# A written order for five engines from the beginning to the first half layer, a folded projection, and lists of the other experts made later

## The chip, the cores and the metric

The kernel runs on one core of a Trainium2 chip. The time is that of one launch in device microseconds; the figure before is the median of three runs. TensorE is written PE, its weight loads PEld, VectorE DVE, ScalarE ACT, GpSimd POOL; SP is the queue that issues most of the transfers.

## The reference

`x` has 2048 tokens of 448 values. The layernorm of it, `xn`, feeds two branches, and the sum of both and of `x` is the output.

```
xn  = layernorm(x)
q   = (xn @ wq) as 16 heads of 28;  k = xn @ wk;  v = xn @ wv     # one key and value head of 28
A   = softmax(q k^T * 28**-0.5) v  ->  (2048, 448) @ wo
gates = softmax(xn @ wg)                    # 8 experts, the best 2 of each token, renormalized
B   = sum over its 2 experts of gate * (gelu(xn @ w1[e]) @ w2[e])  # 448 -> 1792 -> 448
out = x + A + B
```

## The kernel before

All products are carried out in parts: an operand is split into a rounded high part and the low remainder (`hi` on ACT, `lo` a subtraction on DVE or POOL), and a product of 448 rows is 11 matmuls: high by high 4, high by low 3, low by high 4 (`mm11`; the low parts of the last 64 rows ride in the free half of the fourth chunk).

**Prologue.** Sixteen tiles of 128 tokens are loaded (tiles `xn`), normalized (`norm`: statistics on DVE, square root and scaling on ACT, every fourth tile's scaling on POOL), written to DRAM for the gathers (`xn_d`), transposed on PE (L559) and split into `xh` and `xl`. Four tiles make a chunk of 512 tokens. For each chunk `project` multiplies by `wa`, the 64 columns of wk, wv and wg (L581, L583: 7 matmuls of 512 columns, high and low part side by side in 128 columns), copies the result (`pkv`), transposes it back (L588) and adds the two halves into `kvg`. `q_mm` makes a group of four heads, padded from 28 to 32 rows each (L54, 11 matmuls of 512 columns); there are 16 such groups, split by `q_out` and written to DRAM (`q_d`). The tiles are loaded first, then wq in four pieces.

**The gate.** From `kvg` DVE finds the two best experts of each token and counts ranks (`gate_rank`, a count by PE, L361 and L363); the lists of tokens of all eight experts are made at once: `gate_hot` makes one-hot rows `ob` and right-hand sides `rt` of 40 columns (DVE), `gate_tok` multiplies them (L403, 4 groups of 8 matmuls), the result is `tok`. Expert 0's rows are then gathered from `xn_d`, transposed (L240) and split.

**Experts.** An expert has 512 to 576 rows, in two halves (the second takes what is over 256). First layer: 14 steps `f` of 11 matmuls (for a first half 256 columns), gelu on ACT (`gf`, L891), split into `gg` (L35, L899). Second layer: for each group `k` of 128 rows 14 steps of 3 matmuls (L940) with `w2h` and `w2l`, the split pieces of w2. Between these steps `tock` lets in bursts of attention scores: 7 matmuls of 512 columns (L135) into `ps_s` and a half bank `ps_w`, whose maxima DVE takes (`mx`, L152), part of them from ACT's copy `cp`. Two PSUM tiles `ps_w0` and `ps_w1` take turns for the steps' results. The attention itself follows after the last expert.

**What sets the order.** Each engine executes its instructions in the order of the program. Tile, the scheduler, gives that order by priorities; inside a `manual_schedule` the order of the code stands for the engines named. Before, PE, DVE and ACT stand in such an order from the fourth query group to the end of the prologue, and PE from then on; the beginning is Tile's.

The lines that decide which tiles POOL normalizes and how many query groups stand between the projections:

```
moe_attention(..., npool=(3,), hr=50, early=(0, 1, 2, 1))
for ch in range(4):
    if ch < 3:
        norm(ch + 1)
    project(ch)
```

Of the kernel before, what the change touches and what calls it, by code (L numbers as in the profile page):

```python
# [30 lines left out]
EPS = 1e-5  # L31

# [9 lines left out]
def mm11(nc, out, wh, wl, xh, xl, w_is_lhs, between=None):  # L42

# [4 lines left out]
    for i, (a, b) in enumerate(pairs):  # L51
        if not w_is_lhs:
            a, b = b, a
        mm = nc.tensor.matmul(out, a, b, start=i == 0, stop=i == n - 1)  # L54
        if between and i == 2:
            between()
# [4 lines left out]
def moe_attention(ctx, tc, x, wq, wk, wv, wo, wg, w1, w2, out, hp=200, slow=0.4, first=0.9, fin=11, find=4,  # L61
                  npool=(3,), hr=50, early=(0, 1, 2, 1)):
# [7 lines left out]
    q_d = [[dram.tile([512, 512], F32, name=f"q{s}{c}_d") for c in range(4)] for s in "hl"]  # L70
# [16 lines left out]
    tok = cst.tile([128, E * 5], I32, name="tok")  # L87
# [31 lines left out]
    def s_query(t):  # L119
        SQ[t] = sS.tile([128, 4, 128], F32R, name="qs")  # L120
        nc.sync.dma_start(SQ[t].bitcast(F32), q_d[0][t // 4].rearrange("(g p) q -> p g q", g=4)
                          [:, :, (t % 4) * 128:(t % 4) * 128 + 128])
# [78 lines left out]

    def high_w1(pc, st):
# [5 lines left out]
    def low_w1(pc, st, a):  # L208
        b = wp1.tile([128, 4, 256], F32R, name="w1l", tag="w1l")
        lo(nc, b, st, a)  # L210
        W1[0, pc] = a, b

    W1 = {}

    def gather(e, i, xs):
        n = min(128, CAPS[e] - i * 128)
        it = tok[0:n, i * E:i * E + 1] if e == 0 else tokp[0:n, i, e:e + 1]
# [14 lines left out]
    X = {}  # L232
# [4 lines left out]
    def turn_x(e, i, xh, xl, n, xs, p):  # L237
        p = p.rearrange("p (c n) -> p c n", c=4)
        for c in range(4):
            tr = nc.tensor.transpose(p[:, c, 0:n], xs[0:n, c * 128:(c + 1) * 128], ident[0:n, 0:n])  # L240
        s = slice(i * 128, i * 128 + n)
        with tc.high_priority(offset=hp):
            hi(nc, xh[:, :, s], p[:, :, 0:n])
            if e == 0:
                lo(nc, xl[:, :, s], p[:, 0:3, 0:n], xh[:, 0:3, s])
                lo(nc, xh[64:128, 3, s], p[64:128, 3, 0:n], xh[64:128, 3, s])
            else:

                xt = xs.rearrange("p (c n) -> p c n", c=4)
                nc.scalar.activation(xt[:, :, 0:n], p[:, :, 0:n], AF.Copy)  # L250
        if e:
            for o, a, b in ((xl[:, :, s], xt[:, 0:3, 0:n], xh[:, 0:3, s]),
                            (xh[64:128, 3, s], xt[64:128, 3, 0:n], xh[64:128, 3, s])):
                nc.gpsimd.tensor_tensor(o, a, b.bitcast(F32), op=OP.subtract)
        if e == 0:
            trail.append(tr.ins.name)


    with ExitStack() as p0:
# [16 lines left out]

        def load_x(t):
# [978 lines left out]
```

## Time and profile before

| | us |
|---|---|
| median of 3 runs | 1396.79 (1396.76 to 1397.5) |
| profiled execution | 1399.3 |
| its span | 1397.6 |
| PE busy in it | 1366.5 (98%) |
| start to the first matmul of expert 0 | 85.67 |
| first layer of expert 0, first token half | 85.67 to 106.61 |
| second layer of it | 106.61 to 129.77 |

The profiled execution is one run under the profiler, 2.5 us above the median. In the rows, a stretch in square brackets is the idle time before an instruction and what ended it; rows of equal form that follow each other are merged.

### The profile page before, as it was taken

The page shows a single profiled execution, that of the slowest core. Times are in us where ns is not written, and L with a number is a line of the kernel's source. Part 1 is how long each engine was busy: PE and PEld are TensorE (multiplying, and loading weights), DVE is VectorE, ACT ScalarE, POOL GpSimd, SP SyncE. Part 2 cuts the span into 40 slices and gives each one's busy share as a digit, 9 for nine tenths or more (in the row PEclk, how much of TensorE's full clock was granted, in tenths as well). Part 3 has the DMA queues.
Part 4 walks back from the last instruction along what each step waited for, and adds up shares of the span by engine and source line. Part 5 has one row for each costly group of instructions (what it writes and reads, how often), then busy time and mean ns, then how long its engine had stood idle before and what let it go on. Part 6 is the DMA issues. An engine that isn't in the chain of part 4 may idle for free.

```text
span 1397.6 us, 27007 instructions
## 1 busy us (share of the span) xinstructions
PE 1366.5 (98%) x10809; PEld 903.4 (65%) x10809; DVE 753.9 (54%) x775; ACT 997.6 (71%) x1506; POOL 510.7 (37%) x461
## 2 busy tenths in 40 slices
PE   5999999999999999999999999999999999999997
PEld 4887888888788788788788886333333443333333
DVE  6678778778777877788787885211111111111112
ACT  6454674674665665656647645999999999999995
POOL 6010791882872864855838812000000000000000
PEclk9999999999999999999999999999999999999999
DMA  8862251350441341432523314111211122221110
GB/s 263 268 202 82 87 157 34 107 147 30 128 126 37 120 119 51 132 105 66 146 67 107 98 42 110 38 52 51 51 51 51 53 58 61 56 56 51 52 36 23
DMA packets 106495, 124.82 MB, mean 89 GB/s; under 512 B 14914, under 2 KB 94194, under 8 KB 106238
## 3 DMA queue, kind: packets, MB, share of 16 engines
q1 hardware_dynamic: 101278, 106.73, 25.8%
q0 software_dynamic: 5088, 16.32, 4.4%
q8 instruction: 86, 1.41, 0.5%
q14 instruction: 43, 0.35, 0.1%
HBM read 98.25 MB, written 24.77 MB: 88 GB/s over the span
## 4 chain that ended last, share of the span: by engine, by line
PE 92%; DMA 3%; DVE 2%; POOL 1%; ACT 1%; issue 1%; SPq 0%; POOLq 0%; ACTq 0%; DVEq 0%
PE ps_w L54 22%; PE ps_w L940 20%; PE ps_pv L1113 18%; PE ps_s L827 16%; PE ps_s L135 5%; PE ps_s L1035 3%; PE ps_w L135 2%; PE ps_p L54 2%; DMA st<-in_B_w_dram 1%; DMA xs<-xn_d,tokp 1%; PE ps_w L240 1%; PE ps_s L54 1%; POOL w1l L199 1%; PE ps_st L827 1%; DVE mx L152 0%
## 5 line engine op out<-in xcount | busy, mean ns | idle before, releaser
L152 DVE TENSOR_REDUCE mx<-ps_s 128x4 f32<-128x2048 f32 (+1 forms) x159 | 358.5, 2256 | 84.3 <-PE ps_s L135 83.9
L1105 ACT ACTIVATE P<-ps_s 128x512 f32<-128x512 f32 x510 | 282.5, 616 | 33.1 <-PE ps_st L827 28.6
L940 PE MATMUL ps_w<-w2h,gg 128*128 128x448 f32 (+1 forms) x966 | 293.7, 379 | 0.0
L143 ACT ACTIVATE cp<-ps_s 128x1024 f32<-128x1024 f32 x156 | 160.0, 1025 | 159.8 <-PE ps_s L135 125.6
L1113 PE MATMUL ps_pv<-P,vaug 128*32 128x512 f32 x2040 | 269.1, 604 | 0.0
L1105 ACT ACTIVATE P<-ps_st 128x1024 f32<-128x1024 f32 x255 | 268.9, 1055 | 0.0
L899 POOL TENSOR_TENSOR gg<-gf,gg 128x512 fp32r<-128x512 f32 (+2 forms) x140 | 147.4, 1065 | 280.6 <-ACT gg L35 259.2
L940 PEld LDWEIGHTS ps_w<-w2h,gg 128*128 128x128 f32 (+1 forms) x966 | 170.1, 186 | 45.4 <-issue 29.8
L1021 POOL DMA_INDIRECT yk<-y_d,slot x32 | 35.1, 1098 | 431.3 <-DVE xr L1026 424.5
L940 PE MATMUL ps_w<-w2l,gg 128*128 128x448 f32 (+1 forms) x518 | 189.9, 367 | 0.0
L152 DVE TENSOR_REDUCE mx<-cp 128x2 f32<-128x1024 f32 (+1 forms) x157 | 188.8, 1203 | 1.7 <-ACT cp L143 1.7
L827 PEld LDWEIGHTS ps_s<-qah,kT 32*128 32x128 f32 x514 | 47.6, 181 | 207.0 <-ACT P L1105 187.3
L54 PE MATMUL ps_w<-xeh,w1h 128*128 128x256 f32 (+2 forms) x896 | 165.8, 298 | 0.7 <-ACT gf L891 0.7
L54 PE MATMUL ps_w<-xeh,w1l 128*128 128x256 f32 (+2 forms) x896 | 147.8, 287 | 0.0
L54 PEld LDWEIGHTS ps_w<-xeh,w1h 128*128 128x128 f32 x896 | 128.9, 188 | 28.8 <-issue 19.0
L827 PE MATMUL ps_s<-qah,kT 32*128 32x512 f32 x514 | 128.5, 495 | 0.8 <-ACT P L1105 0.5
L827 PE MATMUL ps_st<-qah,kT 32*128 32x512 f32 x510 | 127.5, 495 | 0.0
L54 PEld LDWEIGHTS ps_w<-xeh,w1l 128*128 128x128 f32 x896 | 125.8, 188 | 0.0
L199 POOL TENSOR_TENSOR w1l<-st,w1h 128x1024 fp32r<-128x1024 f32 x49 | 117.3, 2400 | 8.4 <-ACT w1h L35 6.6
L54 PE MATMUL ps_w<-xel,w1h 128*128 128x256 f32 (+2 forms) x672 | 120.0, 287 | 0.0
L135 PE MATMUL ps_s<-kT,qs 28*128 28x512 f32 x939 | 115.2, 452 | 3.0 <-ACT mt L114 1.6
L891 ACT ACTIVATE gf<-ps_w 128x512 f32<-128x512 f32 (+2 forms) x145 | 74.1, 511 | 58.7 <-PE ps_w L54 55.1
(273 smaller groups left out, 2014.7 us busy)
## 6 DMA issues: line engine op xcount, KB each, us to landing
st<-in_B_w_dram SPq DMA_DIRECT2D x56, 448.0 KB
st<-in_B_w_dram SPq DMA_DIRECT2D x52, 384.0 KB
y_d<-y SPq DMA_DIRECT2D x32, 224.0 KB
st<-in_B_w_dram SPq DMA_DIRECT2D x104, 64.0 KB
xn_d<-xn SPq DMA_DIRECT2D x16, 256.0 KB
qh_d<-qh SPq DMA_DIRECT2D x16, 256.0 KB
ql_d<-ql SPq DMA_DIRECT2D x16, 256.0 KB
qs<-qh_d SPq DMA_DIRECT2D x16, 256.0 KB
```

What stands on the lines that cost most here:

```text
L54: mm = nc.tensor.matmul(out, a, b, start=i == 0, stop=i == n - 1)
L135: nc.tensor.matmul(p3 if k < 0 else p[:, k, :] if k < 4 else p2[:, k - 4, :], SQ[t][r, g, :], kT4[r, c * 512:(c + 1) * 512], start=True, s ...
L143: nc.scalar.activation(cp[:, 0:n - k - 4], p2[:, 0:n - k - 4], AF.Copy)
L152: r = V.tensor_reduce(MX[0][:, o:o + z - a], q[:, a:z], axis=AX.X, op=OP.max)
L199: (nc.gpsimd if e else V).tensor_tensor(b, st, a.bitcast(F32), op=OP.subtract)
L827: mm = nc.tensor.matmul(ps[j], k[r, ks], q[r].rearrange("p h q -> p (h q)"), start=i == 0, stop=i == 2)
L891: nc.scalar.activation(g[:, 0:2, 0:n] if pair else g[:, f % 2:f % 2 + 1, 0:n], p, AF.Gelu_apprx_tanh)
L899: (nc.gpsimd if e or hf else V).tensor_tensor(gg[:, :, o:o + w], g[:, :, i], gg[:, :, i].bitcast(F32), op=OP.subtract)
L940: mm = nc.tensor.matmul(p[0:m if m == 128 else 2 * m, 0:D], u, w, start=f == 0 and i == 0, stop=f == NF - 1 and i == len(prods) - 1)
L1035: yield nc.tensor.matmul(p[:, 0:D], a[:, h, :], b[:, h, :], start=i == h == 0, stop=i == 2 and h == 3)
L1105: nc.scalar.activation(o, p, AF.Exp, scale=SCALE)
L1113: nc.tensor.matmul(PV[t][32 * hg:32 * hg + 32, :], vaug[:, kt, :], P[:, hg, :], start=kt == 0, stop=kt == NT - 1)
```

## The change

From the first load to the end of expert 0's first half layer the order of PE, DVE, ACT, POOL and SP is now one written list, `PLAN` (406 words; `s.0` is the statistics of tile 0, `q.0.2.1` the second third of a query group, `L.5` a step of the first layer, `wu.4` a low part of w2, `oh.0.1` two of the one-hot products on POOL). With it come these edits:

- Six tiles of x are loaded, then wq, then the other ten.
- `q_d` has 448 rows instead of 512, without padding. A chunk's fourth query group holds 64 rows of q and the 64 of wk, wv and wg (`project` uses `mm11` on columns 384 to 512 of `wq_h` and `wq_l`); `wa` and its 28 matmuls are gone. A tile of queries is loaded by four transfers of 28 partitions instead of one, and the scores' products use 28 or 29 rows.
- The prologue makes expert 0's list alone: 16 columns instead of 32, right-hand sides of 8 columns, 16 one-hot matmuls of 8 columns.
- The lists of the other experts are made within expert 0: POOL makes the one-hot rows (`all_hot`, 32 instructions of 128x128 into bf16 tiles in the place of `xs`), DVE the right-hand sides (`all_right`, 12 instructions of 320 elements), PE multiplies them in the second layer (`all_tok`, 4 groups of 8 weight loads and matmuls of 80 columns, after steps 7 and 13 of the first 128 rows and 5 and 11 of the second), and DVE sums each group (`tokf`).
- POOL normalizes seven tiles instead of four, and makes the low parts of five of the seven pieces of w1, of two of wq, of some `xl` and three `gg`.

```diff
-        for t in range(4):
+        phase.enter_context(tc.manual_schedule(engines={ET.PE, ET.DVE, ET.Activation, ET.Pool, ET.SP}))
+        for t in range(6):
             load_x(t)
...
+                nc.sync.dma_start(stq, wq[c * 128:c * 128 + 128])
...
-            for c in range(4):
-                nc.tensor.matmul(p, wa[:, c, :], xh[:, c, :], start=c == 0, stop=False)
-            for c in range(3):
-                nc.tensor.matmul(p, wa[:, c, :], xl[:, c, :], start=False, stop=c == 2)
...
+            mm11(nc, p, lambda c: wq_h[:, c, 384:512], lambda c: wq_l[:, c, 384:512], lambda c: XH[ch][:, c, :],
+                 lambda c: XL[ch][:, c, :], True)
...
+            (nc.gpsimd if i in (0, 1, 3, 4, 5) else V).tensor_tensor(b, S1[i], A1[i].bitcast(F32), op=OP.subtract)
...
+    def all_hot(g, i):
...
+        for j in (2 * i, 2 * i + 1):
+            c = g * 8 + j
+            nc.gpsimd.tensor_scalar(HW[g][:, j], HW["i"], cb2[:, c:c + 1], None, op0=OP.is_equal)
+
+    def all_right(g):
...
+        V.tensor_tensor(b, bc(cc2[:, c8, None], SH), bc(i40[:, None, :], SH), op=OP.is_equal)
+        V.tensor_tensor(a, b, bc(t128[:, t8, None], SH), op=OP.mult)
+        V.tensor_scalar(b, b, p1[:, 0:1], None, op0=OP.mult)
+
+    def all_tok(g, p):
+
+        for j in range(8):
+            nc.tensor.matmul(p[:, 0:80], HW[g][:, j, :], HW["r", g][:, j, :], start=j == 0, stop=j == 7)
...
+                    hots = () if e or hf else (5, 11) if k else (7, 13)
...
+                    if e == hf == k == f == 0:
+                        all_right(0)
+                        all_right(1)
...
+                    if e == hf == 0 and f in hots:
+                        g = 2 * k + hots.index(f)
+                        all_tok(g, other_psum())
```

PE in the prologue, where a chunk's keys, values and gate come from (`pkv` is the copy that goes back through PE, `ps_p` and `ps_s` are result banks). Before:

```order
L54 MATMUL ps_s<-xh,wq_l 128x512 x4
L581 MATMUL ps_p<-xh,wa 128x512 x4
L583 MATMUL ps_p<-xl,wa 128x512 x3
L54 MATMUL ps_s<-xh,wq_h 128x512 x4
L588 MATMUL ps_t<-ident,pkv 128x128 x4
```

and after:

```order
L76 MATMUL ps_p<-xh,wq_h 128x512 x4
L76 MATMUL ps_p<-xl,wq_h 128x512 x3
L76 MATMUL ps_p<-xh,wq_l 128x512 x4
L666 MATMUL ps_t<-ident,pkv 128x128 x4
L76 MATMUL ps_p<-xh,wq_h 128x512 x4
```

The seven matmuls by `wa` are gone, and the transposes of `pkv` follow a query group.

ACT at the end of the first layer of expert 0 (`gf` is a gelu, `gg` its high part, `w2h` a piece of w2 from its landing place `st`, `cp` a copy of scores). Before:

```order
L891 ACTIVATE gf<-ps_w_1324 128x2x256
L35 ACTIVATE gg<-gf 128x2x256
L35 ACTIVATE w2h<-st 128x896
L891 ACTIVATE gf<-ps_w_1364 128x2x256
L35 ACTIVATE w2h<-st 128x896
L35 ACTIVATE gg<-gf 128x2x256
L891 ACTIVATE gf<-ps_w_1410 128x2x256
```

and after:

```order
L825 ACTIVATE gf<-ps_w_1243 128x2x256
L61 ACTIVATE gg<-gf 128x2x256
L61 ACTIVATE w2h<-st 128x896 x3
L61 ACTIVATE xeh<-ps_s 128x4x64
L825 ACTIVATE gf<-ps_w_1272 128x2x256
L61 ACTIVATE gg<-gf 128x2x256
L61 ACTIVATE w2h<-st 128x896
```

Three copies of w2 pieces and one of a gathered tile now stand between two of the last gelus.

DVE in the second layer of expert 0 after the second burst (`mx` are the maxima, `w2l` the low part of a w2 piece). Before:

```order
L152 TENSOR_REDUCE mx<-ps_s 128x4
L152 TENSOR_REDUCE mx<-cp 128x2
L152 TENSOR_REDUCE mx<-ps_w_1487 128x1
L794 TENSOR_TENSOR w2l<-st,w2h 128x896
L152 TENSOR_REDUCE mx<-ps_s 128x4
```

and after:

```order
L178 TENSOR_REDUCE mx<-ps_w_1458 128x1
L178 TENSOR_REDUCE mx<-ps_s 128x4
L178 TENSOR_REDUCE mx<-cp 128x2
L844 TENSOR_TENSOR w2l<-st,w2h 128x896 x2
L967 TENSOR_TENSOR gf<-cc_233,i_238 128x8x40 x2
L968 TENSOR_TENSOR gf<-gf,t_239 128x8x40 x2
L969 TENSOR_SCALAR gf<-gf,p_222 128x8x40 x2
L977 TENSOR_REDUCE tokf<-ps_w_1477 128x40
```

The right-hand sides of the other lists (`gf` by L967 to L969) stand behind the second burst's maxima and two splits of w2.

PE at the same place after the change (`L1119` is a step of the second layer, `oh` a one-hot row tile):

```order
L161 MATMUL ps_s_1457<-kT_126,qs 128x512 x2
L1119 MATMUL ps_w_1418<-w2h,gg 128x448 x2
L1119 MATMUL ps_w_1418<-w2l,gg 128x448
L1119 MATMUL ps_w_1418<-w2h,gg 128x448 x2
L1119 MATMUL ps_w_1418<-w2l,gg 128x448
L974 LDWEIGHTS oh_1161
L974 MATMUL ps_w_1477<-gf,oh_1161 128x80
```

Two steps of the second layer stand between the burst's last matmul and the first one-hot product, which needs `gf`.

## Rows read from the trace of the kernel before

**Rows 1.** The page: each engine's busy time with its share of the span and its instructions, and one of the costliest groups (partitions x elements; busy time in all, mean ns of one; idle time before).

```profile
PE 1366.5 (98%) x10809; PEld 903.4 (65%) x10809; DVE 753.9 (54%) x775; ACT 997.6 (71%) x1506; POOL 510.7 (37%) x461
...
L199 POOL TENSOR_TENSOR w1l<-st,w1h 128x1024 fp32r<-128x1024 f32 x49 | 117.3, 2400 | 8.4 <-ACT w1h L35 6.6
```

**Rows 2.** TensorE's waits in the first 130 us: who waited for whom, in all, how often, and the longest.

```profile
PE ps_t L559 <- ACT xn L553: 10.6, 1, 10.6
PE ps_t L559 <- ACT rs L542: 5.1, 1, 5.1
PE ps_p L54 <- DVE ql L39: 1.3, 2, 1.0
```

**Rows 3.** TensorE's timeline, the beginning: start, length of the merged piece (successive pieces overlap a little, so that starts are subtracted), engine, line, operation, count, wait.

```profile
18.49 1.98 PE L559 MATMUL ps_t<-ident,xn 128*128 128x128 f32 x8 [5.06 <-ACT rs L542]
20.26 1.22 PE L581 MATMUL ps_p<-xh,wa 128*128 128x512 f32 x2
...
22.78 0.72 PE L581 MATMUL ps_p<-xh,wa 128*128 128x512 f32 x2
...
24.47 1.09 PE L54 MATMUL ps_s<-xh,wq_h 128*128 128x512 f32 x4
```

**Rows 4.** TensorE's timeline further on, the same columns: the first pieces of two successive runs of 11 query matmuls, the gate's count, one group of eight one-hot matmuls, and what comes next.

```profile
46.26 1.09 PE L54 MATMUL ps_p<-xh,wq_h 128*128 128x512 f32 x4
...
48.82 1.10 PE L54 MATMUL ps_p<-xh,wq_h 128*128 128x512 f32 x4
...
54.03 0.70 PE L363 MATMUL ps_t<-both,one 128*128 128x128 bf16 x16
...
59.81 0.96 PE L403 MATMUL ps_t<-rt,ob 128*128 128x40 f32 x8
60.62 1.18 PE L54 MATMUL ps_p<-xh,wq_h 128*128 128x512 f32 x4
```

**Rows 5.** VectorE's timeline in the prologue: the fourth tile's statistics, a split of wq, the last sum of the projection, the gate's last rank instruction, and a product of 320 elements.

```profile
7.84 0.63 DVE L536 BATCH_NORM_STATS2 st<-xn 128x6 f32<-128x448 f32 x1 [0.87 <-DMA xn<-in_A_x_dram]
...
15.68 0.63 DVE L39 TENSOR_TENSOR wq_l<-stq,wq_h 128x448 fp32r<-128x448 f32 x1 [0.32 <-ACT wq_h L35]
...
45.24 0.42 DVE L592 TENSOR_TENSOR kvg<-ps_t,kvl 128x256 f32<-128x256 f32 x1 [2.13 <-ACT kvl L591]
...
49.74 0.23 DVE L354 TENSOR_TENSOR both<-sel 128x128 bf16<-128x128 bf16 x1
...
57.32 0.49 DVE L394 TENSOR_TENSOR rt<-r,tw 128x320 fp32r<-128x320 f32 x1
```

**Rows 6.** ScalarE's timeline: normalising three tiles, a quarter of the query weights, three copies of transposed tiles, and a copy of a piece of w2 at the end of the first layer.

```profile
9.73 2.07 ACT L553 ACTIVATE xn<-xn,rs 128x448 f32<-128x448 f32 x3 [0.71 <-DMA xn<-in_A_x_dram]
...
15.07 0.58 ACT L35 ACTIVATE wq_h<-stq 128x448 fp32r<-128x448 f32 x1
...
16.72 1.55 ACT L35 ACTIVATE xh<-ps_t 128x512 fp32r<-128x512 f32 x3
...
106.83 0.95 ACT L35 ACTIVATE w2h<-st 128x896 fp32r<-128x896 f32 x1 [0.97 <-DMA st<-in_B_w_dram]
```

**Rows 7.** TensorE's timeline: the first matmul of the first layer of expert 0, the two steps of 11 after it, the first matmul of its second layer, and the first of the other token half.

```profile
85.67 0.72 PE L54 MATMUL ps_w<-xeh,w1h 128*128 128x256 f32 x4
...
87.06 0.64 PE L54 MATMUL ps_w<-xeh,w1h 128*128 128x256 f32 x4
...
88.37 0.64 PE L54 MATMUL ps_w<-xeh,w1h 128*128 128x256 f32 x4
...
106.61 0.57 PE L940 MATMUL ps_w<-w2h,gg 128*128 128x448 f32 x2
...
129.77 0.75 PE L54 MATMUL ps_w<-xeh,w1h 128*128 128x320 f32 x4
```

**Rows 8.** The chain that ended last, one load of a piece of w2 of expert 0: start, length, what.

```profile
102.59 4.21 DMA st<-in_B_w_dram
```

**Rows 9.** VectorE's timeline in the second layer of expert 0: maxima of four banks of scores and of the half bank (those of ACT's copy stand between), and a split of w2.

```profile
110.21 2.29 DVE L152 TENSOR_REDUCE mx<-ps_s 128x4 f32<-128x2048 f32 x1
...
113.54 0.68 DVE L152 TENSOR_REDUCE mx<-ps_w 128x1 f32<-128x512 f32 x1
114.14 1.08 DVE L794 TENSOR_TENSOR w2l<-st,w2h 128x896 fp32r<-128x896 f32 x1
```

**Rows 10.** TensorE's timeline in the second layer of expert 5: a burst's matmuls after a wait, and two steps behind it.

```profile
676.75 0.50 PE L135 MATMUL ps_s<-kT,qs 28*128 28x512 f32 x2 [1.60 <-ACT mt L114]
...
678.83 0.95 PE L940 MATMUL ps_w<-w2h,gg 128*128 128x448 f32 x2
...
679.95 0.95 PE L940 MATMUL ps_w<-w2h,gg 128*128 128x448 f32 x2
```

**Rows 11.** Busy time of each engine by stretch (columns: length, then PE, PEld, DVE, ACT, POOL, the granted clock, the DMA share, GB/s): the second layer of expert 0, first token half, in two parts, and two us of expert 5.

```profile
106.60:117.90 11.30, 10.46 (x58) 7.68 (x56) 10.05 (x9) 5.37 (x7) 0.00 (x0) 1.00 0.55 159
117.90:130.00 12.10, 12.10 (x70) 9.80 (x65) 11.50 (x10) 3.67 (x5) 0.00 (x0) 1.00 0.10 35
678.00:680.00 2.00, 2.00 (x8) 1.77 (x7) 1.22 (x1) 1.07 (x2) 1.92 (x3) 0.52 0.42 106
```

**Rows 12.** GpSimd's timeline: two runs of the same instruction.

```profile
12.08 0.72 POOL L550 TENSOR_SCALAR xn<-xn,rs 128x448 f32<-128x448 f32 x1
...
15.55 1.18 POOL L550 TENSOR_SCALAR xn<-xn,rs 128x448 f32<-128x448 f32 x1 [0.26 <-DVE mv L539]
```

More of the change, by code (lines that the diff above doesn't have):

```diff
@@ L53, in mm11 @@
             a, b = b, a
-        mm = nc.tensor.matmul(out, a, b, start=i == 0, stop=i == n - 1)
+        yield nc.tensor.matmul(out, a, b, start=i == 0, stop=i == n - 1)
+def mm11(*args, between=None):
+    for i, mm in enumerate(mm_steps(*args)):
         if between and i == 2:
@@ L305, in moe_attention, with soon @@
+        for t in range(6, NT):
+            load_x(t)
+        copies = wide()
+        later = []
+        def soon(f, *a, **k):
+            later.append(partial(f, *a, **k))
+        wq_h, wq_l = (wp.tile([128, 4, 512], F32R, name=n) for n in ("wq_h", "wq_l"))
+        soon(nc.gpsimd.memset, vaug, 0.0)
+        soon(nc.gpsimd.memset, vaug[:, :, DH:DH + 1], 1.0)
         ie = to("ie", (128, E))
-        nc.gpsimd.iota(ie, pattern=[[1, E]], base=0, channel_multiplier=0, allow_small_or_imprecise_dtypes=True)
+        soon(nc.gpsimd.iota, ie, pattern=[[1, E]], base=0, channel_multiplier=0, allow_small_or_imprecise_dtypes=True)
@@ new lines, in moe_attention, with turn_rows, part, high @@
+        TP, TC = {}, {}
+        def turn_rows(t):
+            p = TP[t] = psP.tile([128, 4, 128], F32, name="ps_t", bufs=3)
+            for c in range(4):
+                nc.tensor.transpose(p[:, c, :], x_row(t)[:, c * 128:(c + 1) * 128], ident)
+        def part(t):
+            return XH[t // 4], XL[t // 4], slice(t % 4 * 128, t % 4 * 128 + 128)
+        def high(t):
+            xh, xl, s = part(t)
+            hi(nc, xh[:, :, s], TP[t])
+        def copy(t):
+            pc = TC[t] = copies[:, len(TC) % 2].rearrange("p (c q) -> p c q", c=4)
+            nc.scalar.activation(pc, TP[t], AF.Copy)
@@ L728, in moe_attention, with follow @@
+        plan = iter(PLAN.split())
+        def follow(stop=None):
+            for step in plan:
+                if step == stop:
+                    break
+                name, *at = step.split(".")
+                acts[name](*map(int, at))
+        follow("end")
+        assert not later
     mp = pm.enter_context(tc.tile_pool(name="mp", bufs=2, reuse_waits="tile"))
@@ L739, in moe_attention @@
     wt = [0]
+    G1 = [mp.tile([128, 512], F32, name="xs", bufs=3) for _ in range(2)]
+    HW = {}
     def next_psum():
```

646 lines of the change are left out of this document (361 added, 285 removed).

## The prediction

> **What bounds the kernel now.** I read the page first: PE is busy for 98% of the span [rows 1]. What PE gains or loses early therefore passes to the end one for one, unless a later wait absorbs it, and the question is what PE does until expert 0's first half is through. The list of PE's waits in the first 130 us comes next [rows 2]: 15.7 us before PE runs steadily, split in two by a few transposes, then almost nothing. The timeline gives the three stages that the change touches [rows 3, 7]: the prologue to 85.67, the first layer to 106.61 (20.94), the second layer of the first token half to 129.77 (23.16). The table by stretch shows one more thing about the third: DVE is busy for 10.05 of 11.30 and 11.50 of 12.10 us there [rows 11]. It has no room for new work.
>
> The profiled execution was 1399.3 us, 2.5 above the median of 1396.79. I sum against the profiled one and take the difference over unchanged to the median.
>
> **The prologue: what goes.** Before, the chunks' projections cost 28 matmuls of 512 columns, which go since they now ride in columns that were padding. Eleven such matmuls take 48.82 - 46.26 = 2.56 us, 0.233 each [rows 4], so 6.5 us less. Of the four groups of eight one-hot matmuls, 0.81 us each (59.81 to 60.62 [rows 4]), two groups of 8 columns are left, so 1.6 less. Two groups of four transposes more cost 0.9 (eight take 1.77 at 18.49, which I show below to be at half rate, so 0.45 for four [rows 3]).
>
> **When PE can begin.** The steady run starts at 20.26 now, and its first two matmuls take 21.28 - 20.26 = 1.0 us where two at 22.78 take 0.55 [rows 3]: the granted clock at first is half. After the change wq comes behind six tiles instead of sixteen, and tiles of two passes share a wide buffer. The fourth tile lands at 7.8, its statistics take 0.7 [rows 5], and square root and factors end at about 9.3. Then ACT must make two scalings of 0.65 (2.07 for three), four copies of transposed tiles of 0.49 (1.55 for three, with overlap) and four pieces of wq_h of 0.55 [rows 6], with two square roots: 6.1 us, to 15.4, and PE's steady run starts at about 15.8.
>
> **The prologue's sum.** PE's work from there: 176 matmuls of 0.233 = 41.0, 20 groups of transposes of 0.45 = 9.0, the count 0.6 [rows 4], 16 small matmuls 1.6, together 52.2. Half clock for the first 4.2 us costs 2.1. Without any wait the first step of expert 0 starts at 15.8 + 52.2 + 2.1 = 70.1. That is the best case. Before, the stretch from 24.47 to 85.67 held 197 matmuls (45.9), 18 groups (8.1), the count (0.6) and 32 small ones (3.2), 57.8 us of work in 61.2: 3.4 were lost, though PE's listed waits there are only about 1.6, of which DVE's query splits make 1.3 [rows 2]. Hand-overs between five engines don't vanish by being written down, and POOL does more of them now, so I take 3.0 lost again: the first step at 73.1, a gain of **12.6 us** (15.6 at best; 8 if the losses are three times as large).
>
> Does the gate's chain fit in that? DVE's last sum ends at 45.66 and the last rank at 49.97, with one query split of 0.6 between, so 3.65 us of rank [rows 5]. In the new order the last chunk's projection comes first among that chunk's groups and `kvg` is complete at about 44.7, by my estimate, so the count comes at 49.5; the first one-hot product follows 5.8 later as it does now (54.03 to 59.81 [rows 4]), and the list stands at about 56. That leaves 16 us until the first transposed tile is needed at about 72, almost four times the 4.2 of a load of w2 [rows 8]; so this chain is costed at nothing; if that cover went, each microsecond of it would be paid in full. The writes of `xn_d` and the three more transfers for each tile of queries lie on SP and hide behind the same margin; in the attention PE streams the same 512 columns for 28 rows as for 32, so nothing is counted there.
>
> **The first layer.** Fourteen steps of 1.31 us (87.06 to 88.37 [rows 7]) and three groups of transposes give 19.5, 1.4 less than before. But in the new order three w2 copies of up to 0.95 us [rows 6] and a tile's copy stand ahead of the last gelu but one, and their loads, 4.2 us each [rows 8], are issued only as low parts of w2 free their landing places. PE's second layer needs that gelu's PSUM tile back. I expect the 20.94 again: **nil** (1.5 gain at best, 2 lost if a load comes later).
>
> **The second layer: what is added.** The first `all_tok` stands on PE two steps behind the second burst. Its right-hand side is made by DVE behind, in order, that burst's maxima (110.21 to 114.14, 3.93 us in all), two splits of w2 of 1.0 [rows 9] and five products of 0.5 [rows 5]: 8.45 us, while PE has two steps of 0.6, so it waits **7.3 us**. Nothing else is queued on PE that it might do in the meantime: everything behind the waiting weight load is held up, the steps and the bursts, and so in turn ACT's copies and DVE's later maxima.
>
> After such a wait the granted clock is lower. In expert 5, after a wait of 1.60 us, PE's two us from 678 show a granted clock of 0.52 and a step takes 1.12 (678.83 to 679.95 [rows 10, 11]) instead of some 0.6; over three steps that cost about 1.6. I take **1.7** here. The 32 small weight loads and matmuls cost **1.5** (sixteen pairs 0.56 by the count at 54.03 [rows 4], and PE's hand-overs). At the start of the second 128 rows, the PSUM tile that PE wants is the one that DVE has still to reduce for the list, behind another burst's maxima: **2.1** by the same rows. The stretch had 0.84 us of idle on PE (10.46 busy of 11.30 [rows 11]), of which 0.5 falls away. Sum: 7.3 + 1.7 + 1.5 + 2.1 - 0.5 = **12.1 us lost**. From below, DVE's account: 12 products of 0.5 and the sums, 7.3 us, on an engine with 1.85 us free in the stage, so at least 5.5; the chain itself at its shortest (one w2 split fewer, no wait at the second 128 rows) gives 9.5; a second fall of the clock 14.5. I take 12.1, the value of the order as it stands.
>
> **The sum.** -12.6 + 0 + 12.1 = -0.5 us: the profiled execution would be 1398.8 and the median **1396.3**. Gain and loss are large, and they cancel.
>
> A rule of the Trainium skill speaks against the change. The rows first: the same POOL instruction took 0.72 us at 12.08 and 1.18 at 15.55, where DVE's split of wq at 15.68 (two operands in SBUF, 0.63) lies beside it [rows 5, 12]. "SBUF — State Buffer" (section "Who interferes with whom") says that GpSimd and VectorE share a pair of ports by an exclusive lock, held for a whole instruction when VectorE reads two operands in SBUF and GpSimd reads SBUF too. The two rows agree with it, though one pair proves little. By it, the change's shift of work to GpSimd would slow VectorE where it is the bound; the time that it gives is that of the second rival below, worked out there from the rows.
>
> **The rivals.**
>
> *The written order flows, and the wait is short.* The prologue reaches its bound (15.6) and the list's chain is at its shortest (9.5): 6.1 us gained, **1390.7**, or 1391 to 1394 with a part of either. For it: PE's waits before were few [rows 2], so an order with DMA landing in time might cost little. Against it: 3.4 us of unlisted losses before.
>
> *POOL and DVE hold each other up: slower.* The place is the gate's rank and the second layer. A low part of w1 on POOL takes 2.4 us [rows 1]; if it stands in front of the 3.65 us of rank and each holds the other, as 0.72 became 1.18, the rank ends some 2.4 us later and delays query splits on which PE waits, +1.4 after what slack these have. In the second layer `all_hot` is made beside DVE's splits and products, eight of them, each up to 0.3 late: +2.4. That is 3.8 more, **1400.1**; it ends slower by more than can be told from no change as soon as the two delays together pass 3.3 us. For it: the two rows of POOL. Against it: the pair is seen once, and the prologue has spare time on DVE.
>
> *The order does not hold on the chip, or the clock falls twice.* An engine that waits in order holds what is behind it: if SP's list blocks on one write of `xn_d`, or ACT's on one load of w1, every query split behind it is late. At 4 us lost in that way, or a second fall of PE's clock at the second 128 rows (+2) with a slip of the prologue like that of the first (+3): **1400 to 1404**. This is also the case in which the change doesn't do what it is written to do.
>
> **How the numbers follow.** My forecast, gain and loss of about equal size, has 0.40; the flowing order 0.31; the port 0.19; the order that does not hold 0.10. A measurement of this kernel can tell 0.2% from no change, 2.8 us, so "same" is 1394.0 to 1399.6. The forecast's own range is that interval. The range from 1390.0 to 1402.5 takes the first rival up to its best value and the two others but for their ends; about 0.06 is left out on either side. Faster 0.31, same 0.40, slower 0.29.
>
> **What would show it.** In the profile of the changed kernel: the first matmul of expert 0's first layer at 73 (70 to 78); the second layer's first matmul some 21 us later; one wait of PE of about 7.3 us at the first `all_tok`, ended by DVE's product, and behind it a granted clock near one half for a few us; the other token half at 129.3 (129.77 before). If PE shows no wait above 3 us there, the loss is mis-sized and the time is near 1389; if the first step of expert 0 comes after 77, it is the prologue's losses that I have wrong. Nothing from 130 us on should differ by more than one us; if it does, the attention's 28 rows or the four transfers for queries cost what I put at nothing.

## The result, and the profile after

The changed kernel takes 1407.49 us (median of 6 runs, 1403.84 to 1409.22) where the kernel before takes 1396.28 (6 runs beside it): a ratio of 1.0077, 95% interval 1.0063 to 1.0091. It is slower by 11 us, and lies above the range of the prediction. The profiled execution took 1408.38 us, its span 1406.7, 9.1 us more than before. PE's waits up to the other token half, in the changed kernel (line, what it waited for, us in total, times, longest):

```profile
PE ps_t L633 <- ACT xn L619: 8.3, 2, 6.7
PE ps_w L974 <- DVE gf L969: 6.5, 1, 6.5
PE ps_w L1119 <- ACT gf L825: 3.0, 1, 3.0
PE ps_w L1119 <- DVE tokg L977: 2.3, 1, 2.3
PE ps_s L789 <- issue: 2.2, 1, 2.2
PE ps_t L411 <- DVE both L404: 1.1, 1, 1.1
PE ps_w L76 <- DVE tokg L977: 1.0, 1, 1.0
...
```

The wait of 15.7 us at the beginning [rows 2] has shrunk, and six new ones stand behind it. The one of 1.1 us lies in the prologue and is read further below. PE's timeline has the places of the five others: the first step of expert 0, the wait in its first layer, the first matmul of the second layer and three later steps, the step before the first list product, that product and four steps after it, the first matmul of the second 128 rows with two later steps, and the other token half:

```profile
72.79 0.64 PE L76 MATMUL ps_w<-xeh,w1h 128*128 128x256 f32 x4
...
79.11 0.63 PE L789 MATMUL ps_s<-ident,xg 128*128 128x128 f32 x4 [2.24 <-issue]
...
98.15 1.11 PE L1119 MATMUL ps_w<-w2h,gg 128*128 128x448 f32 x2 [3.04 <-ACT gf L825]
...
102.01 0.95 PE L1119 MATMUL ps_w<-w2h,gg 128*128 128x448 f32 x2
...
103.13 0.95 PE L1119 MATMUL ps_w<-w2h,gg 128*128 128x448 f32 x2
...
104.25 0.78 PE L1119 MATMUL ps_w<-w2h,gg 128*128 128x448 f32 x2
...
107.55 0.36 PE L1119 MATMUL ps_w<-w2l,gg 128*128 128x448 f32 x1
114.40 0.71 PE L974 MATMUL ps_w<-gf,oh 128*128 128x80 bf16 x8 [6.49 <-DVE gf L969]
114.91 1.10 PE L1119 MATMUL ps_w<-w2h,gg 128*128 128x448 f32 x2
...
116.18 0.95 PE L1119 MATMUL ps_w<-w2h,gg 128*128 128x448 f32 x2
...
117.30 0.95 PE L1119 MATMUL ps_w<-w2h,gg 128*128 128x448 f32 x2
...
118.39 0.56 PE L1119 MATMUL ps_w<-w2h,gg 128*128 128x448 f32 x2
...
123.83 0.67 PE L1119 MATMUL ps_w<-w2h,gg 128*128 128x448 f32 x2 [2.28 <-DVE tokg L977]
...
125.15 0.92 PE L1119 MATMUL ps_w<-w2h,gg 128*128 128x448 f32 x2
...
128.64 0.67 PE L1119 MATMUL ps_w<-w2h,gg 128*128 128x448 f32 x2
...
137.60 0.86 PE L76 MATMUL ps_w<-xeh,w1h 128*128 128x320 f32 x4 [1.01 <-DVE tokg L977]
```

Read as stages, with the same marks as before [rows 7]:

| stage | before | after | difference | forecast |
|---|---|---|---|---|
| to the first step of expert 0 | 85.67 | 72.79 | -12.88 | -12.6 |
| first layer | 20.94 | 25.36 | +4.42 | 0 |
| second layer, first token half | 23.16 | 39.45 | +16.29 | +12.1 |
| the rest of the span | 1267.83 | 1269.1 | +1.27 | 0 |

The rest is 1.8 us more in the attention (861.60 to 1397.60 before, 868.93 to 1406.70 after) and 0.5 less in the experts. The table by stretch of the changed kernel's first and second layer (columns as in [rows 11]) tells what the second layer's 39.45 us are made of:

```profile
72.79:98.15 25.36, 20.09 (x167) 19.50 (x165) 18.86 (x33) 16.37 (x27) 15.03 (x15) 0.99 0.56 182
98.15:137.60 39.45, 29.67 (x150) 22.16 (x150) 28.91 (x38) 9.63 (x12) 17.55 (x25) 0.79 0.20 58
```

PE idles for 9.8 us there, and the 29.67 that it is busy are stretched: the mean granted clock is 0.79. DVE has 28.91 us of work in a stage that was 23.16 us long.

The two new waits of the first layer are read from the engines that PE waits for. VectorE around the first, changed kernel:

```profile
72.94 1.25 DVE L445 TENSOR_TENSOR g<-rk,th 128x160 f32<-128x160 f32 x1
74.23 0.32 DVE L446 TENSOR_REDUCE ca<-g 128x32 f32<-128x160 f32 x1
74.58 3.00 DVE L447 SCALAR_TENSOR_TENSOR cb<-ca,rk 128x32 f32<-128x32 f32 x1
77.51 0.18 DVE L448 SCALAR_TENSOR_TENSOR cc<-ca,ik 128x32 f32<-128x32 f32 x1
77.72 1.89 DVE L65 TENSOR_TENSOR ql<-ps_p,qh 128x512 fp32r<-128x512 f32 x3
```

GpSimd beside it:

```profile
71.61 2.41 POOL L748 TENSOR_TENSOR w1l<-sx,w1h 128x1024 fp32r<-128x1024 f32 x1 [5.04 <-ACT w1h L61]
74.15 0.97 POOL L246 DMA_INDIRECT xg<-xn_d,tok  x1
75.14 2.39 POOL L748 TENSOR_TENSOR w1l<-sx,w1h 128x1024 fp32r<-128x1024 f32 x1
```

The instruction of 128x32 elements at 74.58, whose like takes 0.18 in the next row, ends at 77.58, when GpSimd's low part of w1 does (77.53); the one at 72.94 ends at 74.19, behind the low part before it (74.02). Three query splits, which read PSUM, stand in order behind them and end at 79.61; PE's transposes begin at 79.11. The profile names no engine for their wait ("issue"), so that they wait for these splits is a reading here, which the first experiment tests. ScalarE at the second wait:

```profile
91.27 0.95 ACT L61 ACTIVATE w2h<-st 128x896 fp32r<-128x896 f32 x1
95.15 0.95 ACT L61 ACTIVATE w2h<-st 128x896 fp32r<-128x896 f32 x1 [2.93 <-DMA st<-in_B_w_dram]
96.39 0.95 ACT L61 ACTIVATE w2h<-st 128x896 fp32r<-128x896 f32 x1 [0.29 <-DMA st<-in_B_w_dram]
97.25 0.37 ACT L61 ACTIVATE xeh<-ps_s 128x256 fp32r<-128x256 f32 x1
97.51 0.59 ACT L825 ACTIVATE gf<-ps_w 128x512 f32<-128x512 f32 x1
```

The gelu at 97.51 frees the PSUM tile that the second layer needs. Its input was ready before 92.4, but three copies of w2 stand ahead of it, and two of them wait for their loads.

### The profile page after: what moved, and what is told of

Its sections match the earlier page's. It is cut to its first block, busy times and chain, and to the rows that moved or that the text cites. A ratio compares the mean times of both kernels' runs of the same rounds, so it can differ in the third digit from the quotient of the medians.

```text
span 1406.7 us, 27128 instructions
## 1 busy us (share of the span) xinstructions
PE 1369.0 (97%) x10797; PEld 902.5 (64%) x10797; DVE 753.7 (54%) x785; ACT 997.6 (71%) x1504; POOL 554.0 (39%) x510
## 4 chain that ended last, share of the span: by engine, by line
PE 94%; DMA 2%; DVE 2%; issue 1%; ACT 1%; POOL 0%; SPq 0%; ACTq 0%; POOLq 0%; DVEq 0%
PE ps_w L76 22%; PE ps_w L1119 22%; PE ps_pv L1304 18%; PE ps_s L1019 16%; PE ps_s L161 5%; PE ps_s L1226 3%; PE ps_w L161 3%; PE ps_p L76 1%; PE ps_w L268 1%; DVE mx L178 1%; PE ps_st L1019 1%; DMA xn<-in_A_x_dram 1%; DMA xs<-xn_d,tokp 1%; PE ps_s L76 1%; DMA qh_d<-qh 1%
## 5 line engine op out<-in xcount | busy, mean ns | idle before, releaser
L1119 PE MATMUL ps_w<-w2h,gg 128*128 128x448 f32 (+1 forms) x966 | 296.9, 383 | 5.3 <-ACT gf L825 3.0
L1119 PEld LDWEIGHTS ps_w<-w2h,gg 128*128 128x128 f32 (+1 forms) x966 | 171.9, 188 | 51.9 <-issue 30.6
L1119 PE MATMUL ps_w<-w2l,gg 128*128 128x448 f32 (+1 forms) x518 | 191.0, 369 | 0.0
L1019 PEld LDWEIGHTS ps_s<-qah,kT 29*128 29x128 f32 x514 | 48.1, 181 | 206.3 <-ACT P L1296 190.0
L1019 PE MATMUL ps_s<-qah,kT 29*128 29x512 f32 x514 | 128.2, 494 | 0.5 <-ACT P L1296 0.5
L1019 PE MATMUL ps_st<-qah,kT 29*128 29x512 f32 x510 | 127.3, 496 | 0.0
L1081 ACT ACTIVATE gf<-ps_w 128x512 f32<-128x512 f32 (+2 forms) x140 | 71.2, 508 | 60.3 <-PE ps_w L76 55.9
```

The lines of the kernel that those rows point to most:

```text
L1019: mm = nc.tensor.matmul(ps[j], k[r, ks], q[r].rearrange("p h q -> p (h q)"), start=i == 0, stop=i == 2)
L1081: nc.scalar.activation(g[:, 0:2, 0:n] if pair else g[:, f % 2:f % 2 + 1, 0:n], p, AF.Gelu_apprx_tanh)
L1119: mm = nc.tensor.matmul(p[0:m if m == 128 else 2 * m, 0:D], u, w, start=f == 0 and i == 0, stop=f == NF - 1 and i == len(prods) - 1)
```

## The experiments

Each theory's numbers were written down before its run. "From the first step to the other half" is the first plus the second layer, 64.81 us in the profile above and 44.10 before. In diffs of the plan only the words around the edit are shown.

**The columns of the other lists later.**

```diff
-wh.5 co qh.3.0 wl.5 kw.3 q.3.2.3 qh.3.1 ql.3.1 qh.3.2 ql.3.0 ql.3.2 va.3
+wh.5 qh.3.0 wl.5 kw.3 q.3.2.3 qh.3.1 ql.3.1 qh.3.2 ql.3.0 ql.3.2 co va.3
```

> Only the place of one step in the written order changes: the columns of all experts' lists (four instructions of VectorE, one of which took 3.00 us where its like take 0.2) stand behind the last three query splits instead of ahead of them. Theory 1 (GpSimd's low part of w1 held VectorE up, and the three splits behind it held TensorE's transposes): TensorE's wait of 2.24 us in the first layer of expert 0 falls below 0.5, the long instruction stays long but holds nobody, and the other token half starts some 2 us earlier; the wait of 3.04 us before the second layer stays. Theory 2 (the transposes wait for gathered rows): the 2.24 us stay.

Measured: 1403.16 us (1402.62 to 1404.37). The wait of 2.24 us is gone, one of 0.5 for a gelu stands a little later, and the wait at the second layer stays with 2.7. From the first step to the other half it takes 62.3 us, 2.5 less. VectorE in this run:

```profile
74.33 1.89 DVE L65 TENSOR_TENSOR ql<-ps_p,qh 128x512 fp32r<-128x512 f32 x3 [2.55 <-ACT qh L61]
...
77.00 0.19 DVE L447 SCALAR_TENSOR_TENSOR cb<-ca,rk 128x32 f32<-128x32 f32 x1
```

Theory 1 holds, and one thing is better than it said: the instruction isn't long here at all, 0.19 us, since GpSimd's low part (74.01 to 76.42 in this run) is over. The three splits, which read one operand from PSUM, ran beside that low part without being held.

**The gelu ahead of the late copies.**

```diff
-S.11 wv.2 wv.3 wv.4 L.12 L.13 gg.4 wu.2 xh.4 ge.5 oh.0.2
+S.11 wv.2 L.12 L.13 gg.4 wu.2 xh.4 ge.5 wv.3 wv.4 oh.0.2
```

> On ScalarE two copies of w2 pieces move from ahead of the last gelu but one to behind it. Theory 1 (the gelu stands in order behind copies that wait for loads): TensorE's wait of 3.04 us at the second layer's start falls below 0.5, and the first four steps there take 0.61 instead of about 1.1 each, since the clock has no reason to fall: 3.0 + 2.2 = 5.2 us gained up to the stall at the first list product. Theory 2 (the loads themselves are late, whoever waits for them): the wait comes back a few steps later, and less than 2 us are gained.

Measured: 1403.12 us (1399.11 to 1403.82), 62.0 us from the first step to the other half, 2.8 less instead of 5.2. The wait at the gelu is gone and the first layer takes 22.15. But PE's first burst then waits 1.98 us for a split of gathered rows, which stands on DVE behind a low part of w2, whose load is late, and the clock falls all the same. It is theory 1 on a second engine: what waits is again work that stands in order behind a load.

**The first right-hand side early.**

```diff
-                        all_right(0)
                         all_right(1)
...
-L.12 L.13 gg.4 wu.2 xh.4
+L.12 L.13 gg.4 wu.2 ar.0 xh.4
```

> VectorE makes the first list's right-hand side (three instructions) within the first layer, where it was idle for 2.6 us, instead of behind the second burst's maxima. Theory 1 (the stall of 6.49 us is VectorE's order, and the slow steps after it are the price of the stall): the wait at the first list product falls below 1 us, the three steps behind it take 0.61 instead of 1.16, and the other token half starts 6.5 + 1.65 = 8 us earlier. Theory 2 (VectorE has no room in the stage, whatever the order): TensorE waits later, at a burst or at the second list product, and 3 us or less are gained.

Measured: 1401.61 us (1400.85 to 1402.66), 59.9 us from the first step to the other half, 4.95 less. Its first product comes without a wait, as theory 1 said; then a burst waits 2.2 us for a list's sum, and the second list product 2.9. The profile names GpSimd's one-hot rows for the latter, but the product came at 117.39, right behind VectorE's last instruction for its right-hand side (116.79 to 117.25), and the eight rows of this list are among the ten that GpSimd had begun by 110.6. The truth lies between: order took 5 us, and 5 us of waits came back, the size of VectorE's missing room.

**Filler in the stall.**

```diff
-                        all_tok(g, other_psum())
+                        pw = other_psum()
+                        for _ in range(0 if g else 30):
+                            nc.tensor.matmul(pw[:, 0:D], gh, a, start=True, stop=True)
+                        all_tok(g, pw)
```

> TensorE gets 30 matmuls of 448 columns, whose result is thrown away, directly ahead of the first list product: some 6.1 us of work in the 6.49 us that it waits there. Theory 1 (the granted clock falls after the wait because TensorE stood idle): the product comes when it came before, and the three steps behind it take 0.61 us instead of 1.16, 1.65 us gained in all. Theory 2 (the list's 8 small matmuls bring the clock down): the steps stay at about 1.1 and the time is the same.

PE's timeline in that run: the filler, the list product, the two steps after it, and the first matmul of the second 128 rows with two steps behind it.

```profile
106.83 6.24 PE L1138 MATMUL ps_w<-w2h,gg 128*128 128x448 f32 x30
113.47 0.45 PE L974 MATMUL ps_w<-gf,oh 128*128 128x80 bf16 x8 [0.41 <-DVE gf L969]
113.75 0.65 PE L1119 MATMUL ps_w<-w2h,gg 128*128 128x448 f32 x2
114.24 0.36 PE L1119 MATMUL ps_w<-w2l,gg 128*128 128x448 f32 x1
114.44 0.57 PE L1119 MATMUL ps_w<-w2h,gg 128*128 128x448 f32 x2
...
121.11 0.67 PE L1119 MATMUL ps_w<-w2h,gg 128*128 128x448 f32 x2 [2.30 <-DVE tokg L977]
...
121.83 0.57 PE L1119 MATMUL ps_w<-w2h,gg 128*128 128x448 f32 x2
122.23 0.36 PE L1119 MATMUL ps_w<-w2l,gg 128*128 128x448 f32 x1
122.44 0.56 PE L1119 MATMUL ps_w<-w2h,gg 128*128 128x448 f32 x2
```

Theory 1: the product comes as long after the second layer's start as before (16.1 us, 16.25 in the changed kernel), and the steps behind it take 0.7 and 0.6 us instead of 1.3 and 1.1. More than expected, the wait of 2.3 us at 121.11 isn't followed by slow steps either, where the changed kernel lost another 1.5 us in that way; this need not be the filler's doing, for in the run with the columns later the clock stays whole behind the same wait too. From the first step to the other half 61.45 us, 3.4 less, which is no more than the changed kernel itself varies by (next run). The runs spread widely (1397.77 to 1405.97, median 1403.61), so what the filler shows is the clock behind the stall, and no gain in time.

**The changed kernel again.**

> The changed kernel itself, unedited, beside the other three of this group, since its six times spread from 1403.8 to 1409.2 and the start of its first layer was 72.8 in one profile and 71.5 to 71.9 in four edits that leave the prologue as it is. Theory 1 (the prologue's start varies by a microsecond from run to run, with when x lands): the first layer starts between 71.5 and 73 and the median lies at 1404 to 1408. Theory 2 (the first profile is typical and each edit of the order moves the prologue): 72.8 again and 1407.5.

Measured: 1404.40 us (1404.20 to 1408.73), 7.5 above the kernel before in its group (1396.95), the first step at 71.84, 61.4 us from there to the other half. The start varies as theory 1 says. More varies than that: here the clock fell after the wait of 2.2 us in the first layer (half in 79.5 to 83), so PE came later to the wait for the gelu (0.8 instead of 3.0) and no second fall followed. Differences of 3 us between single profiles of this kernel are within this scatter; the experiments above are read by their waits first.

**Both edits of the first layer.**

```diff
-gg.4 wu.2 xh.4 ge.5 oh.0.2 wu.3 xl.4 gg.5
+gg.4 wu.2 xh.4 ge.5 wv.3 wv.4 oh.0.2 xl.4 wu.3 gg.5
```

beside the move of the columns above.

> Both edits of the first layer together, and a third that the second of them showed to be needed: the splits of the last gathered tile stand on VectorE ahead of the low part of a w2 piece whose load is late. Theory 1 (the whole surplus of the first layer is work that stands in order behind something late): from the first step to the second layer's first matmul 21 us instead of 25.4, no half clock in the first steps of the second layer; the other half starts 2.2 + 3.0 + 2.2 = 7.4 us earlier than in the changed kernel, counted from the first step (57.4 instead of 64.8). Theory 2 (loads of w2 come late for everyone): a wait of 2 us stays somewhere in the first six steps, 60 us.

Measured: 1403.22 us (1400.59 to 1404.44). The first layer takes 20.73 us, as theory 1 said and as before the change. The second takes 39.5: its second burst waits 2.4 us for the last gelu, which stands behind the next copies of w2, and the list product then 7.3. With 60.2 us in all it is theory 2's number, by theory 1's mechanism at one more place.

**Without the lists of the other experts.**

```diff
-                    hots = () if e or hf else (5, 11) if k else (7, 13)
+                    hots = ()
...
+        V.memset(tokf, 0.0)
```

> The lists of experts 1 to 7 are left out (their one-hot rows, right-hand sides, products and sums; each of their entries is token 0). It shows what the lists cost where they now stand. Theory 1: the stall of 6.49, the two waits for the sums of 2.28 and 1.0, 1.5 of products, and two falls of the clock of 1.65 and 1.9 go, 14.8 us: 50 us from the first step to the other half, median near 1393. Theory 2 (DVE's maxima would hold TensorE there anyway): 8 us or less.

Measured: 1396.11 us (1390.74 to 1400.60). From the first step to the other half 54.9 us, 9.9 less: between the theories. The waits at the products and sums are gone, while the first layer's stay (2.2 and 3.1), PE waits 1.8 us for a low part of w2, and two falls of the clock remain (97 to 103 and 111 to 117). So the lists cost some 10 us where they stand, and even without them the two layers take 10.8 us more than before the change.

**Every edit of order together.**

```diff
-                    hots = () if e or hf else (5, 11) if k else (7, 13)
+                    hots = () if e or hf else (5, 8) if k else (7, 10)
```

beside the edits of the first layer, the early right-hand side, and `oh.1.0` to `oh.1.3` in the plan ahead of `gg.6`.

> The edits of the first layer, the first list's right-hand side in the first layer, the second list's one-hot rows on GpSimd ahead of its last low part (it stood idle for 8.2 us there), and the four list products after steps 7 and 10 of the first 128 rows and 5 and 8 of the second, ahead of the bursts behind which their sums stood. Theory 1 (every loss was one of order): no wait above 1 us from the first step to the other half, 52 us for it, and a median of 1392 to 1396, at or below the kernel before. Theory 2 (VectorE has only 1.85 us to spare and 7.3 to do): 5 us of waits stay, at bursts, with a fall of the clock; a median of 1398 to 1400.

Measured: 1400.84 us (1397.14 to 1402.06). From the first step to the other half 52.4 us as theory 1 says, but with waits of 3.9 us at the second list product and 1.7 for the last gelu (the profile names GpSimd's rows for the first, but those of this list were done at 98.5; VectorE's last instruction for the product ended at 105.25, and the product came at 105.40), and a fall of the clock from 106.4 to 113.4. The median is above both theories: the other half starts 6.4 us earlier than before the change in the profile (whose execution took 1397.14), and the runs' median is 4 us slower than the kernel before all the same. In the profile 2.9 us of that are lost in the later experts (two waits of a burst for ScalarE's `mt`, 2.7, and a fall of the clock at 764) and 1.3 in the attention.

**The kernel before with 28 and 29 rows.**

```diff
-                r = slice(32 * j, 32 * j + 32)
+                r = slice(32 * j, 32 * j + DH + (i == 0))
```

> The kernel before, with one edit of the change alone: the attention's score products take 28 or 29 of the 32 rows instead of all 32. In the changed kernel and its edits the attention, from its first product with the values to the end, takes 537.3 to 538.5 us where it took 536.0 before. Theory 1 (the odd numbers of rows cost TensorE a little at each change): 537.5 to 538.5 us for the attention, and a median 1.5 to 2.5 us above the kernel before. Theory 2 (the difference is scatter, or the loads of queries in four pieces): 536 us, the same time.

Measured: 1397.30 us beside 1396.20, a ratio of 1.0006, interval 0.9997 to 1.0015. Its attention takes 537.46 us, PE busy for 529.59 of them, where the kernel before has 536.00 and 527.57. That is the size that theory 1 said, but the interval of the time takes in no difference, so it stays open whether the rows cost this 1 to 2 us. In the last run below, with the same rows, the attention takes 536.94 us.

**The best version.**

```diff
-            return 0.203 * (3 if m == 128 else 2)
+            return 0.203 * (3 if m == 128 else 2) * (0.6 if e == hf == 0 else 1)
...
-                    hots = () if e or hf else (5, 11) if k else (7, 13)
+                    hots = () if e or hf else (1, 5, 9) if k else (7,)
...
-                        g = 2 * k + hots.index(f)
+                        g = k + hots.index(f)
```

beside the edits of order above, with `ge.6` ahead of `wv.3` and `gg.6` ahead of `oh.1.0` in the plan.

> The combination of the edits so far, and three more for what was still waited for in it: the last gelu on ScalarE ahead of the late copies of w2 pieces, the second list's product a step after the second 128 rows have begun (the others after steps 7, 5 and 9), and fewer bursts in this stage (its steps count for 0.6 in the pacing), so that VectorE has room for the lists and the bursts come later. Theory 1 (VectorE's order and room are all that was left): no wait above 1 us between the first step and the other token half, no fall of the clock there, 46 us for it, and a median of 1391 to 1395, below the kernel before by 2 to 5 us. Theory 2 (bursts put off come back later at a full price): the other half starts as early, but the experts behind it take 4 us longer, 1397 to 1399.

Measured: **1387.20 us** (1386.01 to 1387.45), a ratio of 0.9936 to the kernel before, interval 0.9923 to 0.9950: 9 us faster than before the change and 17 to 20 faster than the change (1404.40 and 1407.49). Its two layers by stretch:

```profile
70.38:90.87 20.49, 20.06 (x168) 19.64 (x166) 15.20 (x33) 14.81 (x25) 14.03 (x14) 1.00 0.66 218
90.87:116.64 25.77, 22.52 (x143) 17.27 (x141) 22.95 (x33) 9.22 (x11) 20.42 (x27) 1.00 0.33 106
```

The clock stays whole, the two layers take 46.3 us (46 expected) with 24 score matmuls in them instead of 34, and what was put off isn't paid again: the rest of its span is 1267.66 us. One wait above 1 us is left, against the expectation, 2.3 us for a low part of w2.

**The best version with all bursts in the stage.** The edit of the pacing is undone.

> The best version with the pacing of bursts put back as it was, so that all bursts of the second layer stay in it; all edits of order stay. Theory 1 (VectorE's room decides, 7.3 us of new work on an engine with 1.85 to spare): 4 to 6 us of waits return between the first step and the other half, 50 to 52 us instead of 46.3, and the median is 3 to 6 us above the best version's 1387.2. Theory 2 (order alone decides): 47 us and 1388.

Measured: 1392.91 us (1391.88 to 1397.14), a ratio of 0.9982 to the kernel before, interval 0.9971 to 0.9993, 51.8 us from the first step to the other half, with a wait of 4.1 us for a low part of w2, one of 1.5 at a list product and a fall of the clock at 104. Around that wait VectorE is busy for 13.68 of 13.72 us (94.04 to 107.76). Theory 1 holds: 5.7 us for VectorE's room, the fall of the clock among them.

**Fewer bursts alone.** The edit of the pacing on the changed kernel.

> The changed kernel with the pacing alone: the steps of this stage count for 0.6, so that the second burst comes behind the first list product. Theory 1: VectorE's queue ahead of the product is shorter by a burst's maxima (3.9 us), so TensorE's stall falls from 6.5 to 3.5 us or less; the waits of the first layer stay; 57 to 60 us from the first step to the other half, median 1399 to 1402. Theory 2 (without the order nothing is gained): the stall stays above 5 us, 1403 or more.

Measured: 1393.41 us (1391.97 to 1397.27), a ratio of 0.9984 to the kernel before, interval 0.9974 to 0.9993: 11 to 14 us less than the change as measured twice (1404.40 and 1407.49), better than either theory. The two layers take 54.8 us. The stall at the first product is 4.6 us, more than theory 1 said; but the waits for the sums are 0.3 us where they were 3.3, the clock falls once in the second layer where it fell three times, and the wait for the gelu is 0.6 in this profile. One line of pacing makes up for all that the change had lost.

## Why the prediction was wrong

**The prologue's sum came out, one of its terms by luck.** 73.1 was forecast, 72.79 came, and 70.4 to 72.6 in the other runs of the written order, down to its bound of 70.1. The steady run began at 15.86 for 15.8. Its first seven query matmuls took 0.42 us each (16.60 to 19.57) instead of 0.233, the half rate of the forecast, although the table by stretch gives a granted clock of 1.00 for 16 to 20 us. But the gate's chain was put at nothing and cost 1.10 us. The first gathered rows were there in time; what PE waited for, in order, was the rank, and this wait lies within the lump of 3.0 us that was taken for hand-overs. The rank's first subtraction, its like later in the same rank, the low part of w1 on GpSimd beside it, and PE's wait:

```profile
45.71 2.09 DVE L396 TENSOR_TENSOR k<-kvg,gm 128x128 f32<-128x128 f32 x1
...
49.52 0.29 DVE L396 TENSOR_TENSOR k<-e,gm 128x128 f32<-128x128 f32 x1
```

```profile
45.25 2.41 POOL L748 TENSOR_TENSOR w1l<-st,w1h 128x1024 fp32r<-128x1024 f32 x1 [1.58 <-ACT w1h L61]
```

```profile
51.10 0.23 PE L411 MATMUL ps_t<-both,up 128*128 128x136 bf16 x1 [1.10 <-DVE both L404]
```

The subtraction ends at 47.80, when the low part does (47.66), and the rank takes 5.65 us (45.39 to 51.04) instead of 3.65. This is the second rival's hold-up at the place that it named, for which it had estimated 1.4 us. It stands in every profile of the written order (2.03 to 2.18 us for the subtraction, 1.08 to 1.42 for PE's wait), that of the best version among them, and no experiment took it out.

**The step that failed first is the first layer, forecast at nil.** The prediction saw the three w2 copies ahead of a gelu and their late loads, and put the effect at 1.4 us, to be covered by what the layer had gained. It is 3.0. And it looked for the lock between POOL and DVE at the gate's rank, where it is, and in the second layer, where it held the other engine, but not at the four column instructions that the plan puts beside a low part of w1: 2.24 us. That moving the columns makes the instruction 0.19 us long, and PE's wait vanish, shows it. In the second layer one of GpSimd's one-hot rows took 2.30 us, where the median of the 24 is 0.61, beside two splits of w2 that kept their time on VectorE, and PE did not wait for it:

```profile
110.22 2.08 DVE L844 TENSOR_TENSOR w2l<-st,w2h 128x896 fp32r<-128x896 f32 x2
```

```profile
110.39 2.30 POOL L957 TENSOR_SCALAR oh<-iob,cb 128x128 bf16<-128x128 f32 x1
```

So the second rival's mechanism cost PE 1.10 and 2.24 us, 3.3 of the 3.8 that it had estimated, one of the two at a place that it had not named. The Trainium skill's rule, "SBUF — State Buffer" (section "Who interferes with whom"), agrees with these rows on both sides: the VectorE instructions that were held read two operands in SBUF, and the three query splits with one operand in PSUM, beside a low part in the run with the columns later, weren't held. At the rank GpSimd's instruction starts first, in the second layer VectorE's. At the columns the rows don't tell who began: GpSimd's low part starts at 75.14 there, behind the instruction that it held.

**The second layer's own terms were right.** The stall is 6.49 for 7.3; the list's matmuls 1.55 (0.51, 0.46, 0.29 and 0.29) for 1.5; the wait for the list's sum at the second 128 rows 2.28 for 2.1. The last wait of 1.01, for the last sum, was left out.

**The clock was counted once and fell three times.** 1.7 us were in the sum for one fall behind the stall, and that one cost 1.6 (three steps in 3.48 us instead of 1.9). The fall behind the wait for the gelu costs 3.0 (four steps and a burst in 6.10 us from 98.15, where the same took 3.31 before, from 106.61 [rows 7] to 109.92, and 0.2 in the step after), and the one behind the wait for the sum 1.5 (two steps and a burst in 3.49 us from 125.15 instead of some 2.0). A second fall stood in the third rival only, with a chance of 0.10. The table by stretch gives a granted clock of 0.50, the lower of the two levels, from 98 to 104, from 112 to 118 and from 126 to 128 us. The kernel before, at the end of the stretch of 3.31 us:

```profile
109.92 0.57 PE L940 MATMUL ps_w<-w2h,gg 128*128 128x448 f32 x2
```

So 16.29 is, to 0.1, the 12.1 forecast, 3.0 and 1.5 for the two falls not counted, 1.0 for the last wait and 0.2 for the one before it, less 0.8 for the shorter stall and some 0.6 for what two bursts of the kernel before had lost (a wait of 0.83, of which the forecast had taken off 0.5, and some 0.3 at the other). The filler shows that the fall behind the stall follows from PE's idle time: the five profiles with an idle stall of 6.5 to 7.3 us all have slow steps behind it, and with work in the stall the steps are at full rate. This agrees with the Trainium skill's "TensorE: Matmul & The Clock Gate" (Part 1: the HAM clock gate), by which activity is what releases the throttle. For the two other falls the same cause is likely but not shown, since waits of 2.2 and 2.3 us are followed by a fall in some profiles and not in others.

**What the chances had wrong** is that cases were held apart that come together: an order that holds up an engine at a few places, and a clock that can fall after each of them. Against the forecast the profile is 9.6 us longer: 4.4 in the first layer, 4.2 in the second, 1.3 in the rest, and 0.3 less in the prologue.

**What decides the stage is VectorE's room**, which the prediction had as its lower bound of 5.5 us: with every edit of order made, 5.7 us more are needed when the bursts stay (the pair of the best version and the one with all bursts). That the change itself goes from 1404.4 or 1407.5 to 1393.4 by putting off bursts fits with this: the order hurts most where the queue on VectorE is long. Not shown: how much of the scatter from run to run is the clock's, and whether 28 rows cost the attention its 1 to 2 us.

## What to carry to other kernels

Work moved into a stage is paid there by the engine that is full: DVE was busy for 21.55 of 23.4 us [rows 11], and 7.3 us of new work cost more than 12 us until the bursts that filled it were put off to where it has room. In an order written by hand, look on each engine for short work behind an instruction that waits for a load or for another engine; such an inversion costs its wait, and the falls of the clock after such waits cost another 1.5 to 3 us here. Idle time on a full TensorE is to be counted with the fall of the clock that may follow it, each time. And a forecast that comes out in sum is still to be taken apart: a wait of 1.10 us lay hidden in a lump for losses.

## What had not been expected of the hardware

A VectorE instruction of 128x32 elements took 3.00 us instead of 0.19 beside one GpSimd instruction of 2.39 us, and one of 128x128 took 2.09 instead of 0.29 beside another of 2.41: what a hold-up costs goes by the other engine's instruction, not by the size of the one held. The clock is not steady in the same place of the same program: after a wait of 2.24 us in the first layer it fell in one profile of the changed kernel and not in another, and after the wait of 2.3 us for the list's sum it fell in the changed kernel, but neither in the run with the filler nor in that with the columns later.
